# A recurrence and a feed-forward layer on one core: free PSUM banks, sums of halves on GpSimd, another order of stages

## The chip, the cores and the metric

The kernel runs on one core of a Trainium2 chip. The core has five engines, each with its own queue of instructions: TensorE (PE; its weight loads are shown apart as PEld), VectorE (DVE), ScalarE (ACT), GpSimd (POOL) and SyncE (SP), which here only issues DMAs. An engine works through its queue in order; semaphores make it wait for others. PSUM, where TensorE writes its results, has eight banks of 512 float32 values per partition.

The metric is the device time of one execution in microseconds: the median of the runs shown.

## The reference

The first part is a recurrence over 768 time steps, for 4 batches and 8 heads of width 48:

```python
for t in range(S):
    cur = np.einsum('bhd,bhe->bhde', u[None] * kt, vt)
    y[:, :, t] = np.einsum('bhd,bhde->bhe', rt, state + cur)
    state = wt[:, :, :, None] * state + np.einsum('bhd,bhe->bhde', kt, vt)
```

Its output, as 3072 rows of 384 values, goes through a feed-forward layer of width 1024:

```python
h = x @ w_in
e = np.exp(h - h_max)
solu = h * (e / np.sum(e))
ln = (solu - mean(solu)) / np.sqrt(var(solu) + 1e-06) * g_ln
return ln @ w_out
```

All inputs and the output are float32.

## The kernel before

The work is cut into 24 units: 6 chunks of 128 time steps times 4 batches (unit i has chunk i // 4 and batch i % 4). A unit goes through stages, each a small function; a stage has a short name, and one string, `ORDER`, names all stages of all units in the order in which they are recorded, with a suffix for the engine (`a` ScalarE, `d` VectorE, `p` GpSimd) or for the place in PSUM. A class `InOrder` keeps each engine's instructions in exactly that order. So each engine's queue is its part of the string, and nothing else decides the order. As the instructions are recorded in the helper, nearly all of them have its line, 87, in the profile; tile names tell the stages apart.

The stages of a unit, with the tile that each writes:

- `LW`, `LK`, `LR`, `LV`: four loads of 192 KB each, on SP, into rings of seven buffers.
- `lw`: the logarithm of the decay (ScalarE, tile lw). `cum`: two matmuls that cumulate it over the chunk (cum_ps). `ex`: its exponential, in place (ScalarE). `kp`: scaled k and r (VectorE).
- `p`, `q`: r times k times u (GpSimd). `dg`: their sum over each head (VectorE). `vb`: v as bfloat16. `dv`: v times that sum (GpSimd), the bonus of the present step.
- `krk`, `krr`: transposes (kr_ps); `kr`: their copy. `M`: scores (m_ps); `m`: their copy, on VectorE with the causal mask `keep` multiplied in, on ScalarE without, and then `sel` masks on GpSimd.
- `Y`: attention within the chunk and on the state (y_ps); `y`: its copy, on VectorE with dv added; where the copy is ScalarE's, `Y` adds dv by one more matmul (suffix `i`). `S`, `et`, `st`: the state for the next chunk.
- `X`, `xT`: the row block transposed. `H`: 24 matmuls of the hidden layer (h_ps, two banks). `e`: exponential (ScalarE). `he`: h times e (VectorE). `hq`: its square.
- `Oa`, `Ob`: the two halves of the output (o_ps). Each of the eight slices of the hidden width takes three matmuls: he with w2 (385 columns; the last sums he), e with a column of constants (one column, the sum of e), hq with a column of ones (one column).
- `sq`, `qm`, `lv`: the factor from these sums; `o`: the scaled output; `out`: its store, on SP.

Ahead of the first output the second weight is made ready: `gw` multiplies w_out by the gain g, slice by slice (w2); `mn` sums the columns by eight matmuls with a matrix of -1/1024 (mean_ps); `mc` copies that mean (mean_sb); `ce` adds it to each slice. So the mean over the hidden width is taken out of the weight. `wi` casts w_in to bfloat16. `hot` is matmuls on a zero tile whose result is not used.

PSUM is taken by tags: `s0` to `s3` of one bank, `b0` and `b1` of two; a stage's suffix names the tag, and a tag's next user waits until its last one is done. The masks and constants are made on GpSimd at the head of the program.

The functions that the change touches:

Of the kernel before, what the change touches and what calls it, by code (L numbers as in the profile page):

```python
# [8 lines left out]
F32 = mybir.dt.float32  # L9
BF16 = mybir.dt.bfloat16  # L10
AX = mybir.AxisListType.X
# [10 lines left out]
LW0 LK0 hot3.s3 LR0 LU0 LG0 lw0 LW1 cum0.b0 LK1 hot1.s3 LV0 LR1 p0 us0.s0 LW2 gs0.s3 hot2.s2 LK2 uc0 gc0 ex0 q0  # L22
LI0 LR2 lw1 kp0 LW3 cum1.b1 hot1.s3 vb0.a dg0 LV1 ex1 S0.s1 LK3 krk0.s2 p1 hot3.s3 LR3 kp1 LI1 lw2 krk1.s0 LI2
krr0 cum2.b0 LV2 kr0.d hot1.s3 LO0 M0.b1 krr1 LO1 m0.d hot3.s3 kr1.a LW4 LK4 p2 et0 ex2 M1.b1 LR4 hot4.s3 LW5
dv0 kp2 lw3 LV3 Y0.is3 m1.d vb1.p LK5 krk2.s2 y0.a q1 LR5 krr2 wi0.a cum3.b0 LW6 S1.s0 q2 dg1 X0.s3 LV4 ex3 st0
dv1 LK6 dg2 kr2.a kp3 LR6 Y1.is1 LW7 y1.a krk3.s2 LV5 et1 wi1.a krr3 X1.s1 LK7 wi2.d M2.b1 LR7 xT1.a p3 xT0.d
m2.d LW8 H0.b0 LV6 vb2.p kr3.d LK8 dv2 H1.b1 e0 st1 LR8 gw3.p LW9 gw0.p he0 S2.s1 LK9 e1 Y2.is3 q3 LR9 hot3.s2
et2 gw2.p LV7 y2.a dg3 gw7.a gw1.p X2.s2 LW10 he1 M3.b0 gw4.p LV8 lw4 gw6.p LK10 m3.d hq0.a gw5.p cum4.b1 LR10
mn0.s0 ex4 LW11 hq1.d LV9 xT2.a p4 kp4 mc0 H2.b0 lw5 ce7.d ce0.d ce3.d ce5.d krk4.s3 vb3.a cum5.b1 ce4.d e2
ce6.d krr4 S3.s2 ce1.d ce2.d st2 dv3 ex5 Oa0.s0 kr4.a q4 kp5 Y3.is1 Ob0 p5 et3 he2 lw6 y3.a krk5.s3 cum6.b1 sq0  # L30
q5 X3.s1 st3 ex6 M4.b0 qm0 krr5 xT3.d vb4.p Oa1.s2 m4.d kr5.a S4.s1 p6 lv0 kp6 M5.b0 o0.a Ob1 dg4 lw7 out0 et4
dg5 krk6.s3 m5.a dv4 cum7.b1 LK11 st4 Y4.ns0 LR11 krr6 hq2.d sq1 vb5.a H3.b0 LW12 ex7 qm1 q6 y4.d LV10 kr6.d lv1
sel5 LK12 Oa2.s1 kp7 e3 LR12 S5.s0 dv5 LV11 o1.a he3 krk7.s3 lw8 M6.b1 out1 vb6.p krr7 et5 m6.a Y5.is2 LW13 p7
kr7.d cum8.b0 LK13 dg6 Ob2 ex8 sel6 LR13 st5 X4.s3 LW14 y5.a kp8 M7.b1 sq2 dv6 xT4.a LK14 X5.s0 Y6.ns2 lw9 qm2
S6.s3 xT5.d LR14 q7 m7.a y6.d krk8.s0 LW15 cum9.b0 hq3.d X6.s2 LV12 krr8 ex9 H4.b1 p8 kr8.d lv2 kp9 et6 sel7
Oa3.s0 vb7.a st6 e4 xT6.d p9 M8.b0 dg7 S7.s3 lw10 he4 krk9.s2 q8 et7 Ob3 m8.a vb8.p o2.d cum10.b1 sq3 sel8 st7
krr9 out2 ex10 S8.s1 qm3 kr9.d LK15 H5.b0 hq4.a q9 kp10 LV13 p10 et8 lv3 st8 M9.b1 e5 krk10.s3 m9.d Y7.ns2 vb9.p
krr10 Oa4.s1 dv7 lw11 he5 o3.a cum11.b1 kr10.a out3 S9.s0 y7.d LR15 H6.b0 et9 ex11 dg8 p11 st9 kp11 Ob4 e6 dg9
X7.s3 krk11.s2 vb10.p lw12 he6 Y8.ns0 dv8 xT7.a krr11 cum12.b1 hq5.a S10.s3 q10 kr11.d H7.b0 sq4 ex12 qm4 y8.d
dv9 dg10 et10 lv4 q11 X8.s2 kp12 Oa5.s0 e7 vb11.p o4.a M10.b1 dv10 he7 Ob5 lw13 out4 xT8.a p12 LW16 S11.s1 m10.a  # L40
dg11 krk12.s2 st10 cum13.b0 et11 hq6.d krr12 sq5 ex13 H8.b1 qm5 sel10 st11 lv5 kp13 lw14 Oa6.s3 q12 e8 kr12.d
krk13.s1 p13 cum14.b0 hq7.a he8 krr13 Y9.ns2 p14 Ob6 ex14 y9.d kr13.a q13 o5.d M11.b1 Oa7.s2 dg12 out5 sq6 dv11
m11.a kp14 LK16 Y10.ns0 vb12.p X9.s1 LR16 qm6 M12.b0 xT9.a M13.b1 LV14 m12.d lw15 Ob7 LW17 m13.a vb13.p S12.s1
LK17 y10.d sel11 cum15.b0 LV15 et12 X10.s0 st12 H9.b1 ex15 dg13 dv12 xT10.a kp15 lv6 Y11.ns1 sq7 e9 krk14.s0 qm7
y11.d H10.b0 hq8.d lw16 o6.a q14 he9 X11.s1 lv7 krr14 out6 Oa8.s3 p15 e10 LR17 xT11.d kr14.d cum16.b1 o7.a dv13
S13.s1 he10 ex16 Ob8 out7 q15 LV16 hq9.a kp16 krk15.s0 sel13 LW18 M14.b0 Y12.ns2 sq8 m14.a dg14 LK18 krr15
H11.b1 qm8 p16 y12.d LR18 et13 lv8 kr15.d LV17 lw17 vb14.p st13 LW19 M15.b0 e11 Y13.ns2 krk16.s0 y13.d Oa9.s1
m15.a p17 he11 X12.s2 vb15.a krr16 sel14 cum17.b0 xT12.a dg15 Ob9 ex17 o8.d dv14 X13.s2 H12.b1 out8 sq9 xT13.a
qm9 kp17 vb16.p lv9 kr16.d H13.b0 e12 hq10.d dv15 o9.a he12 Y14.ns3 lw18 krk17.s2 out9 q16 Oa10.s0 e13 LK19
y14.d sel15 krr17 LV18 Ob10 he13 kr17.a LR19 S14.s1 LW20 hq12.a hq11.d M16.b1 LK20 M17.b0 q17 dg16 Y15.ns3 LR20  # L50
m16.a Oa11.s2 y15.d dv16 sq10 m17.d lw19 cum18.b1 p18 et14 X14.s3 Ob11 xT14.a qm10 st14 lv10 sel16 H14.b0 sq11
ex18 o10.d qm11 vb17.p dg17 out10 lv11 q18 kp18 Y16.ns3 LV19 e14 X15.s1 Oa12.s0 LW21 p19 y16.d xT15.a LV20 dg18
cum19.b1 lw20 Ob12 he14 LK21 q19 ex19 LR21 S15.s3 vb18.p sq12 o11.a LW22 kp19 krk18.s1 dv17 cum20.b0 et15 LK22
krr18 qm12 ex20 X16.s2 p20 H15.b1 out11 xT16.d kr18.a LR22 kp20 LW23 Y17.ns2 lv12 hq13.d H16.b0 e15 st15 y17.d
p21 o12.a S16.s1 he15 e16 out12 krk19.s3 q20 Oa13.s2 LV21 hq14.a he16 LK23 krr19 Ob13 LR23 lw21 kr19.d et16 LV22
X17.s0 M18.b1 st16 M19.b0 p22 S17.s3 m18.d m19.a Oa14.s1 sq13 et17 xT17.a qm13 dg19 cum21.b0 Ob14 st17 ex21
hq15.d krk20.s0 hq16.a Y18.ns3 dv18 kp21 krr20 H17.b1 sq14 lv13 sel19 y18.d lw22 kr20.d lw23 vb19.p Oa15.s3
o13.d e17 vb20.p qm14 dg20 out13 dv19 M20.b0 lv14 LV23 he17 Y19.ns0 m20.a X18.s2 Ob15 xT18.d sel20 o14.d
cum22.b1 sq15 Oa16.s2 y19.d ex22 out14 qm15 hq17.d krk21.s1 vb21.a X19.s0 kp22 q21 Ob16 lv15 q22 xT19.d cum23.b0
sq16 o15.d krr21 ex23 krk22.s0 qm16 H18.b1 p23 out15 kr21.a kp23 dv20 krr22 dg21 e18 S18.s3 kr22.d H19.b0 dv21  # L60
lv16 he18 o16.a Y20.ns1 et18 e19 out16 krk23.s0 hq18.d M21.b1 Oa17.s2 y20.d m21.a st18 krr23 he19 Ob17 sel21
kr23.a Oa18.s1 dg22 sq17 q23 Y21.ns3 hq19.d X20.s0 M22.b1 xT20.a qm17 vb22.p M23.b0 y21.d lv17 Ob18 m23.d dv22
m22.a S19.s0 sq18 X21.s3 dg23 sel22 H20.b1 et19 o17.d xT21.d out17 vb23.p qm18 st19 Y22.ns2 dv23 e20 H21.b0
y22.d lv18 he20 Oa19.s3 e21 o18.d X22.s0 Y23.ns2 hq20.d xT22.a out18 Ob19 y23.d Oa20.s1 sq19 qm19 he21 lv19
X23.s0 H22.b1 xT23.d hq21.a H23.b0 e22 Oa21.s2 he22 e23 Ob20 he23 hq22.a Ob21 sq20 o19.a qm20 hq23.d Oa22.s0
lv20 out19 sq21 o20.d Oa23.s3 qm21 out20 lv21 Ob22 Ob23 sq22 qm22 o21.d lv22 sq23 out21 qm23 o22.d lv23 out22
o23.d out23
# [27 lines left out]
def kernel(  # L95
# [34 lines left out]

    def bank(shape, dtype, slot, name):
        return psum.tile(shape, dtype, tag=slot, name=name)
# [31 lines left out]
    pool.memset(halves, 0.0)  # L164
    pool.memset(halves[0:2, :], 1.0)
    pool.affine_select(out=halves[0:2, :], in_=halves[0:2, :], compare_op=ALU.is_ge, fill=0.0, base=0,
                       pattern=[[1, C]], channel_multiplier=-64)
    pool.affine_select(out=halves[0:2, :], in_=halves[0:2, :], compare_op=ALU.is_gt, fill=0.0, base=64,
                       pattern=[[-1, C]], channel_multiplier=64)
    off_blocks = consts.tile([C, HP, 2], BF16)  # L170
    pool.memset(off_blocks, 0.0)
    pool.memset(off_blocks[0:2], -30000.0)
    pool.affine_select(out=off_blocks[0:2], in_=off_blocks[0:2], compare_op=ALU.not_equal, fill=0.0, base=0,
                       pattern=[[0, HP], [-1, 2]], channel_multiplier=1)
# [10 lines left out]
    for j in range(max(NLW, NKP)):  # L185
        if j < NLW:
            dve.memset(lw_t[j][:, :, D:], 0.0)
        if j < NKP:
# [5 lines left out]
    keep = consts.tile([C, C], BF16)  # L194
    pool.memset(keep, 1.0)
    pool.affine_select(out=keep, in_=keep, compare_op=ALU.is_gt, fill=0.0, base=0,
                       pattern=[[1, C]], channel_multiplier=-1)
# [12 lines left out]
    e_t = ring("e", NWK, [128, KF, C], BF16)  # L210
    he_t = ring("he", NWK, [128, KF, C], BF16)
# [11 lines left out]


# [63 lines left out]
    def centre(f, x):  # L288
        (dve if x == "d" else pool).tensor_add(out=w2[:, f, :DM], in0=w2[:, f, :DM], in1=mean_sb)
# [32 lines left out]

    def v_cast(i, x):
        copy = {"a": act.copy, "p": pool.tensor_copy}[x]
        copy(out=vb_t[i % NLW], in_=v_t[i % NIO][:, :, :D])

    def bonus_sum(i, x):
        dve.reduce_sum(out=dg_t[i % NWK], in_=q_t[i % 3], axis=AX)
# [41 lines left out]
    def scores_mask(i, x):  # L370
        m = m_t[i % NWK]
        pool.affine_select(out=m, in_=m, compare_op=ALU.is_gt, fill=0.0, base=0,
                           pattern=[[0, H], [1, C]], channel_multiplier=-1)

    def attend(i, x):
        L = live[i]
        c, b = units[i]
        m, kr, vb = m_t[i % NWK], kr_s[i % NKP], vb_t[i % NLW]
        y_ps = L["y_ps"] = bank([C, DM], F32, x[-2:], "y_ps")
        first = True  # L380
        if x[0] == "i":
            pe.matmul(y_ps, lhsT=ident, rhs=dv_t[i % NKP].rearrange("t h d -> t (h d)"), start=True, stop=False,
                      skip_group_check=True)
            first = False
        if c > 0:
# [160 lines left out]
```

## Time and profile before

| | us |
|---|---|
| median of three runs | 158.17 (158.06 to 163.34) |
| the profiled execution: its span, the only time that is given for it | 156.5 |
| what the median has beyond that span | 1.7 |
| TensorE busy | 138.6 (89%) |
| VectorE busy | 129.8 (83%) |
| ScalarE busy | 118.4 (76%) |
| GpSimd busy | 103.1 (66%) |
| first output matmul starts | 38.7 |
| last output matmul ends | 152.1 |
| DMA queue of SP | 26.75 MB, 75.4% of 16 DMA engines' span |

The span is from the first to the last instruction. A row of the groups gives busy time and the mean of one instruction from its start to its end; since an instruction may start before the one ahead of it has ended, above all on TensorE, means times counts add up to more than the busy time. "PEclk" is the granted TensorE clock in tenths of full speed. The chain of waits is followed back from the last instruction: at each step what released it, or the instruction ahead of it on its engine.

### The profile page before, as it was taken

To read this page: it belongs to the slowest core of one execution; us is meant where nothing else is said; L and a number is where in the kernel's file an instruction comes from. 1 tells how busy PE (TensorE), PEld (TensorE's weight loads), DVE (VectorE), ACT (ScalarE), POOL (GpSimd) and SP (SyncE) were. 2 spreads that over 40 slices of the span, in tenths; PEclk is the share of its full clock that TensorE was granted. 3 is DMA by queue.
4 is the path that set the end of the run, shared out by engine and by line. 5 is a ranking of instruction groups with operands and counts; after the bars stand their busy time and mean duration, and the time that the engine had idled before them with its cause. 6 is when DMAs were issued, how large, how long until landed. Compare 5 with 4: busy or idle time off the path is not lost.

```text
span 156.5 us, 5279 instructions
## 1 busy us (share of the span) xinstructions
PE 138.6 (89%) x2161; PEld 108.1 (69%) x2161; DVE 129.8 (83%) x227; ACT 118.4 (76%) x241; POOL 103.1 (66%) x131
## 2 busy tenths in 40 slices
PE   3879859449599999999999999999999989999980
PEld 1244447218378788887879788887978778798750
DVE  5054777737999999999989989999999999997652
ACT  4171786616589998989998998999979869655941
POOL 7442858995809999895999977399249782860000
PEclk9999999857999999999999999999999999999999
DMA  4999999999999979999559696596999611011024
GB/s 95 195 215 237 265 354 298 211 226 175 208 224 187 225 155 241 178 228 222 124 121 224 168 194 159 136 211 142 222 212 225 170 57 53 4 50 54 0 105 151
DMA packets 104825, 27.08 MB, mean 173 GB/s; under 512 B 100313, under 2 KB 104418, under 8 KB 104802
## 3 DMA queue, kind: packets, MB, share of 16 engines
q1 hardware_dynamic: 104802, 26.75, 75.4%
q8 instruction: 17, 0.28, 0.7%
q14 instruction: 6, 0.05, 0.1%
HBM read 22.03 MB, written 4.72 MB: 171 GB/s over the span
## 4 chain that ended last, share of the span: by engine, by line
PE 65%; SPq 10%; DVE 9%; POOL 5%; DMA 5%; issue 3%; ACT 1%; DVEq 0%; POOLq 0%
PE o_ps L87 23%; PE h_ps L87 17%; SPq L87 10%; PE kr_ps L87 5%; DMA wout_f<-in_moe_w_out_dram 5%; PE s_ps L87 5%; PE y_ps L87 5%; POOL w L87 5%; PE m_ps L87 4%; PE cum_ps L87 3%; DVE w L87 3%; PE x_ps L87 2%; DVE o L87 1%; DVE hq L87 1%; PE mean_ps L87 1%
## 5 line engine op out<-in xcount | busy, mean ns | idle before, releaser
L87 PE MATMUL o_ps<-w,he 128*128 128x385 bf16 x192 | 45.9, 325 | 1.9 <-DVE w L87 1.9
L87 PE MATMUL h_ps<-xT,win_sb 128*128 128x128 bf16 x576 | 36.5, 222 | 0.7 <-DVE xT L87 0.7
L87 PEld LDWEIGHTS <-win_sb 128*128 128x128 bf16 x576 | 34.0, 99 | 1.1 <-ACT xT L87 0.7
L87 DVE TENSOR_TENSOR he<-h_ps,e 128x1024 bf16<-128x1024 f32 x24 | 29.2, 1217 | 3.1 <-ACT e L87 2.7
L87 PE MATMUL o_ps<-inv_col,e 128*128 128x1 bf16 x192 | 31.7, 165 | 0.0
L87 POOL TENSOR_TENSOR p<-kr_in 128x384 bf16<-128x384 f32 x24 | 24.5, 1023 | 10.9 <-DMA kr_in<-in_r_dram 10.9
L87 PE MATMUL o_ps<-one_col,hq 128*128 128x1 bf16 x192 | 31.3, 163 | 0.0
L87 POOL TENSOR_TENSOR dv<-vb,dg 128x384 bf16<-128x384 bf16 x24 | 20.5, 856 | 13.8 <-DVE dg L87 11.9
L87 ACT ACTIVATE e<-h_ps 128x1024 bf16<-128x1024 f32 x24 | 24.5, 1020 | 6.6 <-PE h_ps L87 6.4
L87 DVE TENSOR_TENSOR kp<-cum_ps,kr_in 128x768 bf16<-128x768 f32 x24 | 22.8, 948 | 7.5 <-ACT cum_ps L87 7.3
L87 PEld LDWEIGHTS <-hq 128*128 128x128 bf16 x192 | 18.5, 96 | 12.8
L87 POOL TENSOR_TENSOR q<-p,u_bc 128x384 bf16<-128x384 bf16 x24 | 23.7, 990 | 1.6 <-DMA kr_in<-in_k_dram 1.5
L87 ACT ACTIVATE cum_ps<-cum_ps 128x768 f32<-128x768 f32 x24 | 19.2, 802 | 3.7 <-PE cum_ps L87 3.4
L87 PEld LDWEIGHTS <-kp 128*128 128x128 bf16 x272 | 17.5, 99 | 3.9 <-DVE kp L87 1.2
L87 PEld LDWEIGHTS <-e 128*128 128x128 bf16 x192 | 18.4, 96 | 2.4 <-issue 2.0
L87 POOL TENSOR_SCALAR_AFFINE_SELECT m<-m 128x1024 bf16<-128x1024 bf16 x14 | 15.7, 1119 | 6.4 <-ACT m L87 4.0
L87 PE MATMUL kr_ps<-ident,kp 128*128 128x128 bf16 x192 | 18.7, 225 | 0.9 <-DVE xT L87 0.5
L87 PEld LDWEIGHTS <-he 128*128 128x128 bf16 x192 | 18.4, 96 | 1.0
L87 ACT CAST m<-m_ps 128x1024 bf16<-128x1024 f32 x14 | 14.2, 1011 | 1.0 <-PE m_ps L87 1.0
L87 DVE TENSOR_REDUCE dg<-q 128x8 f32<-128x384 bf16 x24 | 12.9, 540 | 1.4 <-POOL q L87 1.4
L87 ACT COPY kr<-kr_ps 128x1024 bf16<-128x1024 bf16 x10 | 10.1, 1014 | 4.1 <-PE kr_ps L87 4.1
L87 DVE TENSOR_TENSOR m<-m_ps,keep 128x1024 bf16<-128x1024 f32 x10 | 12.1, 1215 | 0.9 <-PE m_ps L87 0.9
(82 smaller groups left out, 276.4 us busy)
## 6 DMA issues: line engine op xcount, KB each, us to landing
w_in<-in_w_dram SPq DMA_DIRECT2D x24, 192.0 KB, 3.6
kr_in<-in_k_dram SPq DMA_DIRECT2D x24, 192.0 KB, 3.7
kr_in<-in_r_dram SPq DMA_DIRECT2D x24, 192.0 KB, 3.7
v_in<-in_v_dram SPq DMA_DIRECT2D x24, 192.0 KB, 3.6
out_dram<-o SPq DMA_DIRECT2D x24, 192.0 KB, 2.0
win_f<-in_moe_w_in_dram SPq DMA_DIRECT2D x3, 512.0 KB, 5.6
wout_f<-in_moe_w_out_dram SPq DMA_DIRECT2D x2, 768.0 KB, 8.5
u_row<-in_u_dram SPq DMA_DIRECT2D x1, 1.5 KB
```

Source lines behind the costliest of these rows:

```text
L87: made = make(*args, **kwargs)
```

## The change

- PSUM is one tile of eight banks. A stage's suffix is the number of its first bank, and any one or two neighbouring free banks will do. Waits follow from the parts of the tile that are read and written.
- `ce` on VectorE computes a slice anew as w_out times gain plus the mean, which it reads from PSUM; on GpSimd it is as before. Four of the eight slices go to each. The gains go to VectorE (4), ScalarE (2) and GpSimd (2), where seven were GpSimd's.
- `ea`, new, for 17 units: GpSimd adds the upper half of e to the lower (128x512 values), and the output takes four matmuls instead of eight for the sum of e.
- `qh`, new, for 12 units: GpSimd adds the two halves of each head in q (192 values per partition), and `dg` sums half as many.
- `v_cast` may be VectorE's (6 units; 12 GpSimd, 6 ScalarE). The masks are stages in the order (`ih`, `ik`).
- The order is another one: which unit's stage stands where, which engine has which copy (masked scores copies: VectorE 15 for 10; outputs: ScalarE 19 for 11; attention copies: ScalarE 7 for 5), and where loads and stores stand.

```diff
-LW0 LK0 hot3.s3 LR0 LU0 LG0 lw0 LW1 cum0.b0 LK1 hot1.s3 LV0 LR1 p0 us0.s0 LW2 gs0.s3 hot2.s2 LK2 uc0 gc0 ex0 q0
...
-dv1 LK6 dg2 kr2.a kp3 LR6 Y1.is1 LW7 y1.a krk3.s2 LV5 et1 wi1.a krr3 X1.s1 LK7 wi2.d M2.b1 LR7 xT1.a p3 xT0.d
-m2.d LW8 H0.b0 LV6 vb2.p kr3.d LK8 dv2 H1.b1 e0 st1 LR8 gw3.p LW9 gw0.p he0 S2.s1 LK9 e1 Y2.is3 q3 LR9 hot3.s2
...
+LW2 LU0 ik0 lw2 hot5.4 cum2.0 LW1 lw1 us0.7 ih0 LW3 lw3 cum3.2 LR2 uc0 ex2 LK2 p2 LV2 vb2.p kp2 hot4.4 krk2.6 krr2
...
+M4.0 m4.a et1 LI0 S0.5 et0 wi0.d m3.d LO1 wi2.p H1.6 e1 gw5.a H2.0 e2 H0.2 LO0 gw2.a q4 qh4 dg4 qh3 dg3 gw4.p
+gw7.p LV3 vb3.p dv3 sel4 LW6 e0 gw6.d st1 LV4 vb4.p he1 lw6 dv4 gw1.d LW5 gw0.d gw3.d mn0.4 mc0 ce5.p ce6.p
+Y3.i7 ce4.p he2 st0 he0 cum6.0 y3.a ce7.p hot1.5 X3.6 lw5 xT3.a ce3.d LK6 LR6 p6 Y4.n5 LR5 LK5 ce2.d hq0.a ex6
+LW7 cum5.2 H3.6 p5 y4.d ex5 ce1.d ce0.d Oa0.5 kp6 krk6.1 krr6 S4.0 hq1.d Oa1.4 kp5 krk5.3 krr5 X4.2 Ob1 e3 he3
...
+    banks = psum.tile([128, 8 * 512], F32, name="ps")
     def bank(shape, dtype, slot, name):
-        return psum.tile(shape, dtype, tag=slot, name=name)
+        size = 1
+        for d in shape[1:]:
+            size *= d
+        first = int(slot) * 512
+        if dtype == BF16:
+            part = banks[:, first:first + size // 2].bitcast(BF16)
+        else:
+            part = banks[:, first:first + size]
...
     def centre(f, x):
-        (dve if x == "d" else pool).tensor_add(out=w2[:, f, :DM], in0=w2[:, f, :DM], in1=mean_sb)
+        if x == "p":
+            pool.tensor_add(out=w2[:, f, :DM], in0=w2[:, f, :DM], in1=mean_sb)
+        else:
+            dve.scalar_tensor_tensor(out=w2[:, f, :DM], in0=wout_f[:, f, :], scalar=gr[:, f:f + 1], in1=ps["mean"],
+                                     op0=MULT, op1=ADD)
...
+    def bonus_half(i, x):
+        q = q_t[i % 3]
+        pool.tensor_add(out=q[:, :, :D // 2], in0=q[:, :, :D // 2], in1=q[:, :, D // 2:])
...
     def bonus_sum(i, x):
-        dve.reduce_sum(out=dg_t[i % NWK], in_=q_t[i % 3], axis=AX)
+        part = slice(0, D // 2) if i in halved else slice(0, D)
+        dve.reduce_sum(out=dg_t[i % NWK], in_=q_t[i % 3][:, :, part], axis=AX)
...
+    def hidden_add(i, x):
+        e = e_t[i % NWK]
+        pool.tensor_add(out=ea_t[i % NWK], in0=e[:, :KF // 2, :], in1=e[:, KF // 2:, :])
...
-            pe.matmul(o_ps[:, DM + 1:DM + 2], lhsT=e[:, f, :], rhs=inv_col, start=False, stop=False,
-                      skip_group_check=True)
+            if i not in added:
+                pe.matmul(o_ps[:, DM + 1:DM + 2], lhsT=e[:, f, :], rhs=inv_col, start=False, stop=False,
+                          skip_group_check=True)
+            elif f % 2 == 0:
+                pe.matmul(o_ps[:, DM + 1:DM + 2], lhsT=ea_t[i % NWK][:, f // 2, :], rhs=inv_col, start=False, stop=False,
+                          skip_group_check=True)
```

## The prediction

> **What bounds the kernel now.** I read the span in slices first: when is TensorE full, and at which clock?
>
> ```profile
> PE   3879859449599999999999999999999989999980
> DVE  5054777737999999999989989999999999997652
> PEclk9999999857999999999999999999999999999999
> ```
>
> TensorE is full from slice 12 on (45 us) and not before. So there are two terms: when the full stretch begins, and how much work lies in it. Next the busy times of PE, PEld, DVE, ACT and POOL by stretch (length first; then granted clock, DMA share, GB/s):
>
> ```profile
> 38.70:41.90 3.20, 1.31 (x17) 0.87 (x14) 3.20 (x5) 2.27 (x5) 3.12 (x5) 1.00 1.12 218
> ...
> 45.30:117.30 72.00, 71.98 (x1263) 59.94 (x1260) 69.26 (x114) 67.39 (x141) 56.73 (x66) 1.00 0.87 187
> 117.30:126.90 9.60, 9.09 (x148) 7.16 (x146) 9.60 (x19) 8.20 (x19) 8.72 (x10) 1.00 0.71 166
> ```
>
> From 45 to 117 us TensorE rests 0.02 us, but VectorE is at 96%: a second bound close behind, which takes over from 117 to 127. At 39 to 42 TensorE is 41% busy. Why it starts late is in the chain of waits (start, length, what):
>
> ```profile
> 17.12 7.74 DMA wout_f<-in_moe_w_out_dram
> ...
> 24.95 2.46 POOL w L87 x2
> ...
> 29.49 4.91 POOL w L87 x4
> ...
> 34.44 1.13 PE mean_ps L87 x3
> ...
> 36.39 4.85 DVE w L87 x7
> 41.28 0.56 PE o_ps L87 x6
> ```
>
> w_out lands at 24.9, GpSimd multiplies seven of its eight slices by the gain (1.245 us each) until 34.4, TensorE takes the column mean, ScalarE copies it (0.48), VectorE adds it to eight slices. The first output matmul starts at 38.7, but the matmuls wait for slices until 41.3.
>
> **TensorE's work, step by step.** A stage's price is its piece in the full part of the chain: hidden layer 1.34 us, half of the output 0.83, cumulation 0.33, transposes 0.45, scores 0.33, attention 0.37, state 0.46. With these, the order before holds 17.9 us ahead of the first output matmul and 108.3 from it on. The trace took 38.7 to 152.1, 113.4: so 5.1 us are lost there, 1.9 of them waiting for centred slices. One output step in the timeline prices the removed matmuls:
>
> ```profile
> 42.13 0.32 PE L87 MATMUL o_ps<-w,he 128*128 128x385 bf16 x1
> ...
> 42.29 0.17 PE L87 MATMUL o_ps<-inv_col,e 128*128 128x1 bf16 x1
> ...
> 42.31 0.16 PE L87 MATMUL o_ps<-one_col,hq 128*128 128x1 bf16 x1
> ...
> 42.34 0.32 PE L87 MATMUL o_ps<-w,he 128*128 128x385 bf16 x1
> ```
>
> The row says 0.165 us for one column, but matmuls are pipelined: start to start it is 0.026. The change removes 17 x 4 = 68 of them: 68 x 0.026 = 1.8 us, not the 11 us that the row suggests. Two more units add their bonus by an identity matmul (2 x 0.16), two warm-ups go (2 x 0.21). The rest of the gain on TensorE is order: the new one puts H3, two more attentions, a score and a cumulation ahead of the first output and one state behind it, so 19.9 us ahead (2.0 more) and 104.4 from it on: 3.9 less than now.
>
> **When the output can start.** In the new order 18 instead of 15 unit loads are queued on SP ahead of w_out's end. At the saturated 205 GB/s a load of 192 KB is 0.96 us; w_out moves from 24.9 to 27.7 us. The last part of w_in is then there by about 23.4 (2 us start, 18 loads, half of the 8.6 us that remain for the weights out of 24.9), its VectorE copy (0.69) ends at 24.1, and the first hidden layer runs 24.4 to 25.8. On VectorE: exp (1.02, ScalarE) until 26.9, product of unit 1 until 28.1, three gains until 29.3, product of unit 2, a state (0.55), product of unit 0 until 32.2, two centrings, a y (0.55), two centrings: 35.2. ScalarE has hq0 done by 33.7. The mean (gains of ScalarE and GpSimd end by 29.3, eight matmuls at 0.16) is there at 30.7 and is covered. GpSimd starts its four centrings after v, dv and a mask of units 3 and 4, at 33, and ends at 37; they are needed only by the second half of a unit, after Oa0, Oa1 and two transposes (38). I take 36.0 for the first output matmul, 0.8 for semaphores, against 38.7 now, and no wait of 1.9 inside it. If the hidden layers or the masks come late, nothing covers VectorE's chain, and it is 1 for 1 on the end.
>
> Rows that the trace lacks, with ends: a gain on VectorE 0.35 (xT copy) to 0.61 (o), taken 0.4; a centring with PSUM input 0.55 (y) to 0.95 (kp), taken 0.6; on GpSimd 0.86 (dv) to 1.25 (gain), taken 0.99 as q; the w_in cast on GpSimd 0.54 (v) to 1.43 (v by elements), taken 1.4. Together with 1 us either way in the landing of w_out, -1.5 to +2.5 us on the start.
>
> **The other engines.** Sums by row means: VectorE 140.0 now, 138.5 after (15 for 10 masked scores copies +6.1, 5 for 13 outputs -4.9, six v casts +2.4, four gains +1.6, centring -2.5, twelve halved sums -2.9, the rest -1.3). The page has 129.8 for 140.0, as starts overlap ends, a factor 0.927. After the last centring 108.0 are left now (from 41.2) and 105.4 in the new order, from 35.2: an end at 140.6 for VectorE alone, much the same as TensorE's 36.0 + 104.4. ScalarE stays (133.3 to 133.8 by row means). In the built program its separate wait instructions go from 32 to 68, since reads of one bank by two engines are now waited for one by one; between nothing and 0.06 us each that is 0 to 2.2 us, hidden in ScalarE's 24% of idle time. TensorE's 37 waits on its own earlier work go: 0 to 0.55 once (17.5 us), taken 0.
>
> GpSimd takes over 17 sums of e. Ends for one: 0.99 (q has 384 elements, this 512) to 1.32 (q by elements), taken 1.3; and 12 halves of q, 0.29 (a 128x128 cast) to 0.99, taken 0.55. Less five masks, six casts and five gains, it goes from 103 to 124 us. The sum runs beside VectorE's product and square (1.2 + 0.7) and is ready before them if GpSimd is free. Behind it in the queue stand p, q and dv of later units.
>
> The same engine slows VectorE, as the tile view says (min/median/max ns):
>
> ```profile
> L87 DVE TENSOR_TENSOR hq<-he x14: 673/686/1409, 31.1 to 148.5; 128x1024 bf16<-128x1024 bf16 x14
> ```
>
> The 1.41 us one, at 124.3, starts with two q on GpSimd, 2.23 for 0.91 each. Mean 0.82 for 0.68: 2.0 us in all now; with a fifth more on GpSimd and ten more copies and gains exposed, 1 to 3 more, taken 1, in VectorE's slack of about 4.
>
> A rule against the change stands in the Trainium skill, "GPSIMD Engine Reference", Engine selection: elementwise work belongs on VectorE, GpSimd is about twice as slow with two inputs. Its per-element model (2.6 cycles at 1.2 GHz) would make a sum of 512 elements 1.1 us, an estimate from that page: 17 of them 3 us less on GpSimd than I take, and the forecast the same, since it is not on the path.
>
> SP: 40 unit loads now stand ahead of the first store, 44 before. A load behind a store waits for it. The tightest is the v of unit 22 behind the store of unit 12, used 1.4 us of TensorE work later with 3.6 us to land: 2 to 3 us late on GpSimd, with the sums of 16, 18 and 17 behind it. Output 16 comes 7.6 us of TensorE work later, which hides it.
>
> **The sum.** 36.0 + 104.4 + 5.1 lost as now (the 1.9 of waits for slices goes; I put as much for stalls in the first units after it, where VectorE has products, squares and copies of several units queued back to back) = 145.5; tail as now, 156.5 - 152.1 = 4.4; span 149.9. The median of the runs lies 1.7 over the profiled span of 156.5: **151.6 us**.
>
> **Rivals.** *VectorE and GpSimd hold TensorE up*: both are near full, the start slips to 37.5 and twice the stalls (10.2) arise: 37.5 + 104.4 + 10.2 + 4.4 + 1.7 = 158.2. For: the 117 to 127 stretch and the 1.41 us square. Against: 0.02 us of rest over 72 us at 96% of VectorE.
>
> *GpSimd becomes the bound, slower than before*: what it waited for between 45 and 140 us starts
>
> ```profile
> POOL dv L87 <- DVE dg L87: 11.2, 6, 4.5
> POOL p L87 <- DMA kr_in<-in_r_dram: 5.2, 3, 3.0
> POOL m L87 <- ACT m L87: 4.0, 3, 3.0
> ```
>
> and sums to 22.6. After its last centring (37.7) it has 95.3 us left; with the same 22.6 of waits the last sum ends at 155.6, two output halves (1.6), tail and 1.7 follow: 163.3. It decides once the waits exceed 145.5 - 1.6 - 37.7 - 95.3 = 10.9. Against: most of those waits were for want of work.
>
> *The early start does not come*: the first output stays at 38.7, and only the shorter rest remains: 38.7 + 104.4 + 5.1 + 4.4 + 1.7 = 154.3.
>
> **Chances.** Forecast 0.55 (148.5 to 154.0, by the start's ends and 3 to 7 us of stalls), no early start 0.10, held up 0.18, GpSimd bound 0.17. Two per cent, about what a measurement of this kernel tells from no change, is 155.0 to 161.3: faster 0.62, same 0.21, slower 0.17. The range reaches from the forecast's lower end into the held-up case: 148.5 to 160.0.
>
> **What would show it.** Right: first output matmul at 35 to 37, its run without gaps of a microsecond, TensorE full from 42, GpSimd sums of 1.0 to 1.3 us never the releaser of o_ps, output halves of 0.78. Wrong: TensorE waiting for the sum of e or for VectorE in the middle stretch, or w2 ready later than 38.

## The result, and the profile after

The changed kernel takes 154.22 us (median of four runs, 153.98 to 154.78) against 158.24 for the kernel before on the same chip: ratio 0.9748, 95% interval 0.971 to 0.9785. It is faster; 151.6 had been forecast. Medians are over all runs; ratios leave out the runs that were disturbed on the chip, which are four of six for two of the kernels below (the gains alone, and the sums for the last units), so that only the ratio is given there, with a wide interval.

The page's slices of the changed kernel, in the form that was shown for the kernel before:

```profile
PE   6777598968999999999998999999799999999970
DVE  5029968899999999998999999999999999988940
POOL 7268986799909994899999997799889979973600
PEclk9959969999999999999999999999999999999998
```

TensorE is full from slice 10 (38 us) on, but for slices 21 and 28 (80 to 84 and 107 to 110). VectorE is full from slice 8 almost to the end. The clock dips twice ahead of 23 us, where it had dipped from 27 to 39. Now the busy times of PE, PEld, DVE, ACT and POOL by stretch (then granted clock, DMA share, GB/s):

```profile
38.20:42.00 3.80, 3.75 (x57) 2.94 (x57) 3.80 (x4) 3.27 (x5) 3.60 (x4) 1.00 1.09 216
...
45.30:117.30 72.00, 70.45 (x1187) 57.58 (x1185) 70.45 (x116) 65.85 (x144) 65.31 (x74) 1.00 0.96 205
117.30:126.90 9.60, 9.60 (x173) 8.65 (x172) 9.56 (x15) 8.10 (x17) 8.59 (x10) 1.00 0.18 66
```

The first row is the start of the output: 3.75 of 3.80 us busy, where TensorE was 41% busy before. In the 72 us of the middle it now rests 1.55 us (0.02 before), VectorE is at 98% (96%), and the DMA engines are busy for 0.96 of the time at 205 GB/s (0.87 at 187). So three resources stand within a few per cent of each other in the middle stretch.

| | before | after |
|---|---|---|
| profiled execution: span | 156.5 | 152.4 |
| first output matmul starts | 38.7 | 38.2 |
| from there to the end of the last output matmul | 113.4 | 109.4 |
| TensorE's work in it, by the prediction's prices | 108.3 | 104.4 |
| lost in it | 5.1 | 5.0 |
| from there to the end of the span | 4.4 | 4.8 |

The 4.1 us of span are 0.5 at the start and 4.0 behind it, less 0.4 at the tail. The start was to give 2.7. The chain of waits up to it (start, length, what):

```profile
13.35 3.79 DMA kr_in<-in_k_dram
...
19.25 3.19 PE ps L86 x28
...
22.46 1.24 DVE m L86
...
25.59 1.06 ACT win_sb L86
...
26.70 1.47 PE ps L86 x23
28.17 0.02 issue
28.19 1.03 ACT e L86
29.23 0.02 issue
29.25 1.22 DVE he L86
30.47 2.40 DVE w L86 x3
32.87 1.13 DVE he L86
```

The chain no longer passes through w_out's landing, GpSimd's gains and the mean. It runs through the first units' own stages to the hidden layer at 26.7, and then, behind one exponential, on VectorE alone: product, three gains, two more products, centrings. From there VectorE is the path to the first output.

### The profile page after: what moved, and what is told of

It is laid out like the page before. It is cut to its first block, busy times and chain, and to the rows that moved or that the text cites. A ratio compares the mean times of both kernels' runs of the same rounds, so it can differ in the third digit from the quotient of the medians.

```text
span 152.4 us, 5172 instructions
## 1 busy us (share of the span) xinstructions
PE 136.4 (90%) x2093; PEld 105.5 (69%) x2093; DVE 131.8 (87%) x227; ACT 120.0 (79%) x247; POOL 119.0 (78%) x149
## 4 chain that ended last, share of the span: by engine, by line
PE 53%; DVE 23%; SPq 8%; ACT 6%; issue 3%; DMA 2%; POOL 1%; DVEq 0%; POOLq 0%
PE ps L86 53%; SPq L86 7%; DVE he L86 6%; DVE m L86 4%; DVE kp L86 4%; DVE w L86 3%; DMA kr_in<-in_k_dram 2%; DVE kr L86 1%; DVE hq L86 1%; DVE y L86 1%; DVE st L86 1%; ACT ps L86 1%; ACT o L86 1%; DVE dg L86 1%; ACT win_sb L86 1%
## 5 line engine op out<-in xcount | busy, mean ns | idle before, releaser
L86 PE MATMUL ps<-w,he 128*128 128x385 bf16 x192 | 44.5, 325 | 1.0 <-DVE w L86 0.7
L86 PE MATMUL ps<-xT,win_sb 128*128 128x128 bf16 x576 | 35.5, 219 | 1.1 <-DVE qm L86 0.8
L86 PE MATMUL ps<-one_col,hq 128*128 128x1 bf16 x192 | 31.5, 164 | 0.0
L86 DVE TENSOR_TENSOR he<-ps,e 128x1024 bf16<-128x1024 f32 x24 | 29.1, 1214 | 1.6 <-ACT e L86 1.6
L86 DVE TENSOR_TENSOR kp<-ps,kr_in 128x768 bf16<-128x768 f32 x24 | 22.8, 951 | 7.7 <-DMA kr_in<-in_k_dram 4.9
L86 ACT ACTIVATE e<-ps 128x1024 bf16<-128x1024 f32 x24 | 24.5, 1021 | 3.1 <-PE ps L86 2.0
L86 POOL TENSOR_TENSOR ea<-e 128x512 bf16<-128x512 bf16 x17 | 20.0, 1181 | 6.4 <-ACT e L86 5.7
L86 ACT ACTIVATE ps<-ps 128x768 f32<-128x768 f32 x24 | 19.1, 799 | 5.1 <-PE ps L86 4.3
L86 PEld LDWEIGHTS <-he 128*128 128x128 bf16 x192 | 18.4, 96 | 4.0
L86 DVE TENSOR_TENSOR m<-ps,keep 128x1024 bf16<-128x1024 f32 x15 | 18.2, 1216 | 1.2 <-PE ps L86 1.0
L86 PE MATMUL ps<-ident,kp 128*128 128x128 bf16 x192 | 16.5, 227 | 1.6 <-POOL p L86 1.1
```

What stands on the lines that cost most here:

```text
L86: made = make(*args, **kwargs)
```

## The experiments

A first group takes the change apart on the side of the kernel before, a second on the side of the kernel after; a third tries to use what they showed.

### PSUM as one tile

The old order, in the old places of PSUM, with PSUM as one tile:

```diff
-krk0.s2 krr0 cum2.b0 kr0.d M0.b1
+krk0.2 krr0 cum2.4 kr0.d M0.6
```

> The kernel before, its order unchanged; only PSUM is one tile of eight banks, with the old tags on fixed banks (s0 to s3 on 0 to 3, b0 on 4 and 5, b1 on 6 and 7). If the new way of waiting on PSUM costs or gains nothing by itself (my theory): 158.2 within 0.5. If TensorE's 37 waits on its own earlier work cost it something, up to 2 us less, 156.2 to 157.5. If the more numerous ScalarE waits cost: up to 2 us more.

Measured: 158.41 us, ratio 0.9988 [0.9959, 1.0018], no change. The other form of PSUM and of its waits is neither gain nor loss by itself; what matters is the order that it allows.

### The sums of e, in the old order

The kernel before with `hidden_add`, each sum right behind its exponential, in the 17 units that the change names:

```diff
-e5 krk10.s3
+e5 ea5.p krk10.s3
```

> The kernel before, its order unchanged, but for the same 17 units GpSimd adds the halves of e (right after e in the order) and the output takes four matmuls fewer. Theory that the full stretch is TensorE's: 68 x 0.026 = 1.8 us less, 156.4. Rival, that VectorE and GpSimd hold TensorE up: GpSimd gets 17 x 1.18 = 20 us more, slows VectorE's squares and queues ahead of dv, so 158.2 or more.

Measured: 163.7 us, ratio 1.0281 [1.0203, 1.0359]: slower by 4.5 us. In its profile the first output starts at 40.6 instead of 38.7; that is not the sums' work, as the first of them runs at 64.9 (w_out had landed 1.1 us later in this execution). At the 33rd output matmul of 385 columns, at 64.8, it is 1.1 us behind the kernel before, at the last one 5.2. Between the first output and the last one 10.3 us are lost instead of 5.1. The waits of this kernel over the whole span (what waited for what: sum, times, longest):

```profile
POOL ea L86 <- ACT e L86: 9.8, 9, 3.0
...
PE y_ps L86 <- POOL m L86: 1.6, 1, 1.6
...
DVE y L86 <- POOL dv L86: 1.4, 2, 0.9
```

GpSimd works in order. It stands nine times before a sum whose exponential is not there, 9.8 us in all, with the next units' p, q and dv queued behind. TensorE then waits for a masked score of GpSimd (1.6 us) and VectorE for a dv (1.4 us), two waits that the trace of before does not have. The chain of waits runs through GpSimd's sums and bonuses, for instance here:

```profile
64.93 1.15 POOL ea L86
...
66.53 0.79 POOL dv L86
```

This is the mechanism of the forecast's rival "GpSimd becomes the bound", in the old order. That the time is near the rival's price (163.3) is chance: the price was summed up for the new order.

### Gains and centring, in the old order

The kernel before with the gains and the centring on the engines that the change gives them, each in its old place:

```diff
-gw3.p gw0.p gw2.p gw7.a gw1.p gw4.p gw6.p gw5.p
+gw3.d gw0.d gw2.a gw7.p gw1.d gw4.p gw6.d gw5.a
-ce7.d ce0.d ce3.d ce5.d ce4.d ce6.d ce1.d ce2.d
+ce7.p ce0.d ce3.d ce5.p ce4.p ce6.p ce1.d ce2.d
```

and with the new `centre`, which computes VectorE's slices from w_out, gain and the mean in PSUM.

> The kernel before, its order unchanged, but gains and centrings on the engines that the new kernel uses for them (gains: VectorE 4, ScalarE 2, GpSimd 2; centring: VectorE 4 from PSUM, GpSimd 4). Theory that the end follows the first output one for one: the gains end some 3.5 us earlier, the first output without waits starts at 36 to 37 instead of 38.7 with 1.9 of waits, 154 to 155.5. Rival, that VectorE is the bound and the start matters little: it has about 1 us less to do in all, 157 to 158.2.

Measured: 154.25 us, ratio 0.9721 [0.9666, 0.9776]. This part alone gives all that the whole change gives. Its first output starts at 34.19, 4.5 us earlier than before, and its last ends 4.8 earlier. VectorE's weight work in its timeline (start, length, engine, line, operation, shape, count):

```profile
25.06 0.75 DVE L85 TENSOR_SCALAR w<-wout_f,gr 128x384 bf16<-128x384 f32 x2 [0.29 <-DMA wout_f<-in_moe_w_out_dram]
...
31.96 2.17 DVE L85 SCALAR_TENSOR_TENSOR w<-wout_f,gr,mean_ps 128x384 bf16<-128x384 f32 x4
```

The first gains start as w_out lands, at 0.4 each; the centrings are over at 34.1, where the old ones ended at 41.2. The clock, at half from 30.4 to 37.3 us in the kernel before and full here, is at most a small part of this: of the old weight chain only the last three matmuls of the mean run on TensorE in that stretch, for 1.13 us, where all eight take 1.33 here.

The gains alone, with all eight centrings as before:

```diff
-gw3.p gw0.p gw2.p gw7.a gw1.p gw4.p gw6.p gw5.p
+gw3.d gw0.d gw2.a gw7.p gw1.d gw4.p gw6.d gw5.a
```

> The kernel before, its order unchanged, with only the gains spread (VectorE 4, ScalarE 2, GpSimd 2); the mean is still copied and added on VectorE to all eight slices. Theory that GpSimd's 8.6 us of gains were the path: most of the 4.4 us of gains and centring together comes from this part, first output at 35, 155. Rival, that centring from PSUM on two engines is what counts: 157 to 158.

Measured: ratio 0.9746 [0.9648, 0.9845], not separated from the run above; it rests on two runs (153.76 and 155.18) of six that reach 160.05. The profiled execution (156.64) starts its first output at 34.64, but the second slice comes late:

```profile
34.64 0.32 PE L85 MATMUL o_ps<-w,he 128*128 128x385 bf16 x1 [0.59 <-DVE w L85]
...
37.81 0.32 PE L85 MATMUL o_ps<-w,he 128*128 128x385 bf16 x1 [2.82 <-DVE w L85]
```

VectorE adds the mean to the eight slices from 32.7 to 38.0. So the output runs on from 37.8, where the kernel before had 41.3 and the one with both parts 34.2, and the 17th output matmul of 385 columns (47.72) is 1.7 us ahead of before, against 6.2 with both. By this profile the new centring is worth as much of the start as the gains; by the two runs of the ratio the gains alone reach about the same time. How the 4 us are shared stays open.

### Taking parts out of the changed kernel

The changed kernel once more, unchanged, as the measure of the others:

> The new kernel, unchanged, beside the other three: 154.2 again. Its profile shows how far the first output (38.2 us in the first profile, where the granted clock dipped to 0.5 and 0.6 in two early slices) moves from execution to execution: if the dips made it late, 36.5 to 37 without them.

Measured: 154.18 us, ratio 0.9731 [0.9683, 0.9779], first output at 38.16, the last output matmul of 385 columns at 147.23 as in the first profile. The clock dipped again in the same place: 0.56 on average from 18.4 to 21.9 us (0.51 in the first profile). So this run does not show the start without the dip; the next one does.

Without the sums of e:

```diff
-out0 ea5.p Y6.i5
+out0 Y6.i5
```

> The new kernel without GpSimd's sums of e: all units take eight one-column matmuls for the sum again. Theory that TensorE is the bound: 1.8 us more than the new kernel, 156.0. Rival, that VectorE and GpSimd are the bound: GpSimd is relieved of 20 us and VectorE of held squares, 154.2 or less.

Measured: 154.12 us, ratio 0.9714 [0.9667, 0.9762], the same time although TensorE has 68 matmuls more. What this kernel waited for between 45 and 125 us, and two pieces of its chain:

```profile
POOL p L83 <- DMA kr_in<-in_r_dram: 4.8, 3, 3.1
POOL p L83 <- DMA kr_in<-in_k_dram: 3.3, 1, 3.3
POOL vb L83 <- DMA v_in<-in_v_dram: 2.3, 3, 1.7
```

```profile
53.80 4.89 DMA kr_in<-in_r_dram
...
68.37 4.86 DMA kr_in<-in_r_dram
```

The changed kernel has no wait for a load in that stretch; its chain runs through VectorE and ScalarE where this one runs through the loads. The loads in this chain were issued late: SP's issues ahead of the first one begin at 50.9, when a scaled copy has freed a buffer of the ring, and follow each other until 53.8; the load then takes 4.9 us (median of all here: 3.8). How much of that is the rate of the DMA engines and how much the seven buffers of the ring was not separated.

In the profiled execution without the sums the output started 1.2 us earlier (36.97), though the changed kernel has no sum ahead of 56 us. What differs is the granted clock (the third number from the end), here from 18.4 to 21.9 us in the changed kernel and then in this one:

```profile
18.40:21.90 3.50, 3.15 (x28) 2.07 (x28) 2.86 (x4) 1.37 (x3) 3.01 (x5) 0.51 0.98 302
```

```profile
18.40:21.90 3.50, 3.02 (x46) 1.99 (x47) 3.40 (x6) 2.19 (x4) 2.96 (x4) 1.00 0.94 296
```

The 28 matmuls of the changed kernel's chain that start at 19.25 took 3.2 us, the same matmuls 2.2 here. The hidden layer came 0.7 us earlier (26.0), and the three gains behind it took 1.90 us instead of 2.48. So the earlier start goes with the clock of this execution, not with the sums; one profile of each does not tell how often it comes.

Of 192 matmuls with 385 columns, the 17th came 1.5 us ahead of the changed kernel's and the 33rd 0.5 us. No sum's matmul lies between these (the first stands at 60.9 us in the changed kernel), so about 1 us was given back where the chain waits for the load at 53.8; from there on this kernel falls back another 1.4 us, for which the 68 matmuls (1.8) are enough.

Without the halves of the bonus sum:

```diff
-q4 qh4 dg4
+q4 dg4
```

> The new kernel without the halves of q: VectorE sums all 384 values in all units (12 x 0.2 = 2.4 us more for it), GpSimd has 6.5 us less. Theory that VectorE is the close second bound: 154.2 to 156. Rival, that GpSimd's queue is the bound: 153 to 154.

Measured: 154.15 us, ratio 0.9723 [0.9673, 0.9772], the same. VectorE is busy for 132.8 instead of 131.8 us, GpSimd for 112.4 instead of 119.0. One engine's microsecond is bought with 6.6 of the other's, and neither is felt.

With the old gains and the old centring in the new order:

```diff
-gw5.a gw2.a gw4.p gw7.p gw6.d gw1.d gw0.d gw3.d
+gw5.a gw4.p gw7.p gw6.p gw2.p gw1.p gw0.p gw3.p
-ce5.p ce6.p ce4.p ce7.p
+ce5.d ce6.d ce4.d ce7.d
```

> The new kernel with the old way of the second weight: seven gains on GpSimd in a row, one on ScalarE, the copied mean added on VectorE to all eight slices. Theory that the whole gain is this part: the first output comes 5 us later, and the time is 158 to 160, no better than the kernel before. Rival, that order, sums and halves bring something of their own: below 157.

Measured: 162.5 us, ratio 1.0235 [1.0178, 1.0293]: slower than before. GpSimd's queue in its timeline, and what VectorE then waited for:

```profile
27.37 8.56 POOL L84 TENSOR_SCALAR w<-wout_f,gr 128x384 bf16<-128x384 f32 x7 [2.28 <-DMA wout_f<-in_moe_w_out_dram]
```

```profile
DVE w L84 <- ACT mean_sb L84: 8.2, 1, 8.2
```

Seven gains in a row, 8.56 us, and VectorE stands 8.2 us; the first output starts at 47.4. Part of that is the clock, granted at 0.50 from 34 to 47 us: the eight matmuls of the mean took 2.98 us, where they take 1.49 in the run below that draws the weight path together. So the new order needs the new centring: it puts w_out later, and has nothing else to do while the weight is made ready.

### Is the start on the path one for one?

Three kernels try to start the output earlier. In the changed kernel, three of VectorE's gains put ahead of the product of unit 1:

```diff
-e0 gw6.d st1 LV4 vb4.p he1 lw6 dv4 gw1.d LW5 gw0.d gw3.d mn0.4
+e0 gw6.d gw1.d gw0.d gw3.d st1 LV4 vb4.p he1 lw6 dv4 LW5 mn0.4
```

> The changed kernel with one edit in the order: three of VectorE's four gains (slices 1, 0, 3) stand right behind the fourth (slice 6), ahead of a state and of the product of unit 1. They then run at 28.0 us, where VectorE waits 0.74 us for the exponential anyway, and where GpSimd does its own two gains; in the changed kernel they run at 30.4 beside GpSimd's v cast, bonus and mask and take 2.48 us for three. Theory (GpSimd's work of those kinds makes VectorE's gains slow, and the first output's start is on the path to the end one for one): the three gains take 1.2 to 1.4 us, the product of unit 2 follows that of unit 1 directly, the first output matmul starts at 36.2 to 37.0 instead of 38.2, and the median falls to 152.3 to 153.2. Rival A (any work of GpSimd slows these gains, its gains too): they take 2.4 us again, the start gains 0.4 us or less, the median stays at 154.0 to 154.4. Rival B (the start is not what sets the end, VectorE's total is): the start falls to 36.5 and the median stays at 154.0 to 154.4.

Measured: 153.1 us, ratio 0.9684 [0.9654, 0.9713]. Five of its six runs (152.81 to 153.63) lie below all ten of the changed kernel (153.72 to 154.78); the intervals of the ratios just touch (0.9713 and 0.971). One piece of its chain and the three gains in its timeline:

```profile
19.62 9.79 DMA wout_f<-in_moe_w_out_dram
```

```profile
29.43 1.57 DVE L84 TENSOR_SCALAR w<-wout_f,gr 128x384 bf16<-128x384 f32 x3 [1.09 <-DMA wout_f<-in_moe_w_out_dram]
```

The expectation was half wrong: the gains could not run at 28.0, because the second half of w_out landed only at 29.4. But they took 1.57 us for 2.48: they were over at 31.0, when GpSimd's bonus had just begun (30.87) and its mask had not (31.65). The profile is of the slowest of the six runs (154.16) and has its first output at 37.93, so it does not show where the typical run's 1.1 us are.

In the old order with the new centring, the whole weight path drawn together:

```diff
-gw0.d he0 gw2.a gw7.p gw1.d he1 gw4.p lw4 gw6.d hq0.a gw5.a cum4.b1 mn0.s0
+gw0.d gw1.d he0 gw2.a gw7.p gw6.d gw4.d he1 gw5.a lw4 hq0.a mn0.s0 cum4.b1
-hq1.d kp4 ce0.d ce3.d krk4.s3 krr4 ce1.d ce2.d Oa0.s0
+ce0.d ce3.d ce1.d ce2.d kp4 hq1.d Oa0.s0 krk4.s3 krr4
```

> The kernel before with the changed kernel's gains and centring (that alone gave 154.25 and a first output at 34.2), and now its weight path drawn together in the order: slice 4 is VectorE's too (GpSimd has one gain left), the gains stand ahead of the product of unit 1, the mean's eight matmuls ahead of a cumulation, and VectorE's four centrings ahead of a square and a scaled copy, with the transposes of unit 4 behind the first half of the output. Theory (the end follows the first output one for one): mean at about 28.5 us, VectorE's centrings from 30.7 to 32.9, first output at 33.0, 1.2 us earlier, and 152.8 to 153.4. Rival (VectorE's total, or stages pushed behind the output, hold the rest back): the start falls to 33 and the median stays at 154.0 to 154.6, with the lost time from first output to last matmul going from 4.9 to 6 us.

Measured: 155.79 us, ratio 0.9818 [0.9761, 0.9876], 1.5 us slower by the median than without these moves (0.9721, up to 0.9776, so the intervals just touch); the first output starts at 37.07, later instead of earlier. Its timeline says why:

```profile
33.33 2.19 DVE L85 SCALAR_TENSOR_TENSOR w<-wout_f,gr,mean_ps 128x384 bf16<-128x384 f32 x4 [1.89 <-ACT mean_sb L85]
```

```profile
36.44 0.34 PE L85 MATMUL cum_ps<-lw,uti_neg 128*128 128x384 bf16 x1 [1.97 <-DVE kp L85]
```

Two queues were overlooked. The copy of the mean stood on ScalarE behind an exponential that now came after the mean, and VectorE's centring, though it reads the mean from PSUM and not the copy, started only when the copy ended, by a semaphore of ScalarE's for which it waits in this program. And the cumulation of unit 5, which stands in TensorE's queue ahead of the output, needs the PSUM place that the scaled copy of unit 4 frees, which had been put behind the centrings: 1.97 us of TensorE.

Last, the changed kernel with the three gains early and the product of unit 2 behind the centrings:

```diff
-ce4.p he2 st0 he0 cum6.0 y3.a
+ce4.p he0 st0 y3.a
-hq0.a ex6 LW7 cum5.2 H3.6 p5 y4.d ex5 ce1.d ce0.d Oa0.5 kp6 krk6.1 krr6 S4.0 hq1.d Oa1.4 kp5 krk5.3 krr5 X4.2
+hq0.a LW7 cum5.2 H3.6 p5 y4.d ex5 ce1.d ce0.d he2 Oa0.5 cum6.0 ex6 kp5 krk5.3 krr5 hq1.d Oa1.4 kp6 krk6.1 krr6 S4.0 X4.2
```

> The changed kernel with the three gains put forward as in the run before, and also the product of unit 0 ahead of that of unit 2, which goes behind VectorE's four centrings; the stages that hang on unit 2's bank (cumulation, exponential, scaled copy, transposes of unit 6) go behind the first output. So 1.2 us of VectorE's work leaves the path to the first output, and none of it is removed. Theory (the rest from first output to last matmul is 109.4 us wherever the start lies, so the end follows the start): first output at 36.7 to 37.0, the last output matmul starts at 146.0 to 146.5, median 151.8 to 152.4, against 153.0 with the gains alone put forward. Rival (VectorE is full from 29 to 46 us, and that backlog, not the place of one stage in it, sets the end): the start comes earlier as said and the rest grows by as much, to 110.5; median 152.8 to 153.3. Slower than 153.5 would mean that TensorE now waits in its queue for the stages that were put behind.

Measured: 156.09 us, ratio 0.9867 [0.9835, 0.9899]. The start came as said, at 36.97. The rest grew, and the time with it. Two lines of its timeline:

```profile
38.68 0.80 ACT L84 ACTIVATE ps<-ps 128x768 f32<-128x768 f32 x1 [1.67 <-PE ps L84]
```

```profile
38.98 0.62 PE L84 MATMUL ps<-ident,kp 128*128 128x128 bf16 x8 [0.38 <-DVE kp L84]
```

ScalarE now waits 1.67 us for the cumulation that was put behind, and TensorE for a scaled copy. The 192 output matmuls of 385 columns, in the order of their time, show what became of each start (us, from the timelines):

| matmul | before | gains and centring alone | after | after without sums | gains early | product of unit 2 behind |
|---|---|---|---|---|---|---|
| 1st | 38.69 | 34.19 | 38.20 | 36.97 | 37.93 | 36.97 |
| 17th | 49.44 | 43.22 | 47.25 | 45.75 | 46.83 | 47.50 |
| 33rd | 63.70 | 57.48 | 60.69 | 60.15 | 60.26 | 60.94 |
| 65th | 86.44 | 81.18 | 84.13 | 83.55 | 83.70 | 84.39 |
| 97th | 105.97 | 100.68 | 103.59 | 103.90 | 103.67 | 104.37 |
| 161st | 142.29 | 137.52 | 139.62 | 140.15 | 139.70 | 140.43 |
| 192nd | 151.77 | 147.00 | 147.23 | 148.12 | 147.31 | 148.03 |

With the product of unit 2 put behind, the output is 1.2 us ahead of the changed kernel at the first matmul and 0.25 behind at the 17th, nine microseconds later. The kernels without sums and with early gains lose their advance (1.5 and 0.4) between the 17th and the 97th. The kernel with gains and centring alone is 6.2 us ahead of the kernel before at the 17th and 4.8 at the end, and between 45 and 125 us its longest wait was this:

```profile
POOL p L85 <- DMA kr_in<-in_r_dram: 10.7, 4, 4.5
```

So the theory "the end follows the start one for one" falls. An earlier start counts as long as everything behind it can come earlier too. Beyond that, some of it is given back: where the chain of waits runs through loads (three pieces without the sums, one with gains and centring alone: 4.59 us of a load of the decay at 62.05), or at once to the stages that were pushed aside. Of the last kernel's 3.0 us over the one before it, the two profiles show 0.7 at the last output and 1.1 in the tail; the rest isn't settled, since one of the two profiles is of an untypically slow run.

### Sums where nothing stands behind them

The kernel with gains and centring alone, and sums only for units 20 to 23:

```diff
-e20 H21.b0
+e20 ea20.p H21.b0
```

> The kernel before with the changed kernel's gains and centring, and sums of e on GpSimd for the last four units (20 to 23) alone, each right behind its exponential; behind the first of them GpSimd's queue holds only the last few bonus products. Theory (a sum costs nothing where nothing is queued behind it, and saves four one-column matmuls of 0.026 us): 16 matmuls fewer, 0.4 us, 153.7 to 154.0, against 154.25 without the sums. Rival (a sum of 1.2 us stands between exponential and output and delays the last units, where each stage waits for the one ahead): 154.5 to 155.5.

Measured: ratio 0.9593 [0.9495, 0.9691], from two runs (150.62 and 152.72) of six that reach 156.51. The interval overlaps that without the sums (0.9666 to 0.9776). It speaks against the rival, a loss; that the sums help here by the 0.4 us expected isn't shown.

## Why the prediction was right, and where it was not

**The verdict** was right and the time, 154.2, was in the range, but 2.6 us over the forecast. By its number it is the third rival, *the early start does not come* (154.3, given 0.10): the start moved by 0.5 us and the shorter rest gave the other part. Of the 2.6 us, 2.2 are the start and 0.4 the tail.

**The step that failed is "I take 36.0 for the first output matmul".** It came at 38.2. Three of its terms were too small.

- *The last part of w_in by 23.4, the first hidden layer from 24.4 to 25.8.* It landed at 25.2, and the layer ran from 26.70 to 28.17. The estimate counted loads, and the last one came 1.8 late. It left out the queues: ScalarE's cast of w_in ran only at 25.59, behind two copies of k and r and two of x, the last of which waited for a chain that starts with a load of k at 13.35. And it left out the clock, which was at 0.51 on that chain: in the execution at full clock, with the same landing (25.2), ScalarE's cast ran at 24.54 and the layer from 26.0. So 1.6 of the 2.3 us are the landing and the cast behind it, 0.7 ScalarE's late cast. The prediction's own words, that nothing covers VectorE's chain if the hidden layers come late, name what happened.
- *w_out at 27.7.* Its second half was issued at 19.6 and took 9.6 us, so 29.2; in the run with early gains it ended at 29.4. In the changed kernel that lay under the late hidden layer.
- *Three gains until 29.3, at 0.4.* One took 0.41, the other three 2.48. The timelines of VectorE (its last line is the last of the three by itself) and of GpSimd show them side by side:

```profile
27.63 0.41 DVE L86 TENSOR_SCALAR w<-wout_f,gr 128x384 bf16<-128x384 f32 x1
...
30.39 2.48 DVE L86 TENSOR_SCALAR w<-wout_f,gr 128x384 bf16<-128x384 f32 x3
...
31.62 1.24 DVE L86 TENSOR_SCALAR w<-wout_f,gr 128x384 bf16<-128x384 f32 x1
```

```profile
29.96 0.50 POOL L86 CAST vb<-v_in 128x384 bf16<-128x384 f32 x1 [0.25 <-DMA v_in<-in_v_dram]
30.55 0.94 POOL L86 TENSOR_TENSOR dv<-vb,dg 128x384 bf16<-128x384 bf16 x1
31.45 1.21 POOL L86 TENSOR_SCALAR_AFFINE_SELECT m<-m 128x1024 bf16<-128x1024 bf16 x1
```

The third and fourth gain took 0.99 and 1.24: the last one starts at 31.62, just behind the mask, and ends at 32.86, 0.2 behind the mask's end; the one before it ends as far behind the bonus (31.70 for 31.49). That is 1.3 us more than taken, on the path. The prediction had the effect, as 1 us somewhere in VectorE's slack; it fell where there was none. The run that moves the gains out of GpSimd's way had 1.57 for the three, and 1.1 us less time by its median; its profile, of its slowest run, starts the output only 0.3 earlier, so the link between the two isn't shown. The Trainium skill, "SBUF — State Buffer", SBUF: two separate sides, says that VectorE, in some of its modes, and GpSimd take turns at a pair of ports, each for a whole instruction; the gain that lasts until the mask is over agrees with that. The first gain, 0.41 in the midst of GpSimd's own gain (27.25 to 28.50), was not held, but in the run with early gains another one was: 0.66, ending 0.2 behind GpSimd's gain (30.43 for 30.21). What decides this is not shown.

The first and third miss make 3.6 us. Behind the gains, 0.6 came back, as each of VectorE's instructions starts some 0.08 us ahead of the end of the one before it, which the prediction's sum of durations left out here; and of the 0.8 taken for semaphores 0.05 were needed. That leaves the measured 2.2. The other terms of the step held: centring from PSUM 0.60 (taken 0.6), on GpSimd 0.83 (0.99), ended at 37.7 (37); the cast on GpSimd 1.04 (1.4). There is no wait of 1.9 us inside the first output.

**The rest behind the start** came out as summed, 109.4 for 109.5: work 104.4, lost 5.0 for 5.1. The 5.0 is partly luck: 1.9 of stalls were put in by a guess, for the first units; TensorE rested 0.2 us there, and 1.55 in the middle stretch, which was to be full. The reading of the 3.9 us as a gain was too simple, too. Of them, 2.0 were only moved ahead of the start, where VectorE is the path; what they cost there was not measured. The other 1.8, the 68 removed matmuls, are nowhere in the median: the kernel without the sums is as fast. What the forecast left out is that loads stand close behind in the middle stretch (loads and stores take 0.96 of the DMA engines' time): they are on the chain of the kernel without sums and of the one with gains and centring alone. The new order and the new way with the weight do not add: the second takes the old order to 154.25; the new order with the old way is at 162.5.

**The sums of e and the halves.** A sum took 1.18 on average (taken 1.3), a half 0.55 (0.55). The Trainium skill's model ("GPSIMD Engine Reference", Elementwise — side-by-side cycle accounting) makes 1.1 of a sum, an estimate, near the median of 1.15 here; the mean lies above that by one sum of 1.60 beside VectorE's square. From the tile view, count and min/median/max in ns of the sums, and of VectorE's squares, which run beside them:

```profile
L86 POOL TENSOR_TENSOR ea<-e x17: 1147/1153/1600, 56.1 to 143.1; 128x512 bf16<-128x512 bf16 x17
```

```profile
L86 DVE TENSOR_TENSOR hq<-he x15: 673/772/1581, 38.9 to 144.5; 128x1024 bf16<-128x1024 bf16 x15
```

The squares take 0.89 on average for 0.82 before, 1 us over 15 of them; without the sums they take 0.84. GpSimd is busy for 119.0 us (103.1 before); its durations add up to 123.2, for 124 expected by row means.

**The rival of GpSimd** did not come. What GpSimd waited for between 45 and 140 us:

```profile
POOL ea L86 <- ACT e L86: 5.0, 3, 3.2
POOL dv L86 <- DVE qm L86: 3.6, 1, 3.6
POOL dv L86 <- DVE vb L86: 2.7, 1, 2.7
```

With two smaller ones these sum to 13.3 us, above the 10.9 at which the rival was to decide. (That point takes 37.7 for the end of GpSimd's centrings, the sum for the start 37; it was 37.7.) It did not: the last sum starts at 143.1 and ends 3 us ahead of the last output matmul of 385 columns, and no output waits for one. A wait for an exponential that is itself late with TensorE's path is no load on GpSimd, and the point counted it as one. The mechanism is real, as the sums in the old order show.

**The rival of VectorE** is half there: the chain of waits runs through VectorE and ScalarE at 75 to 83 and 90 to 110 us, and TensorE rests 1.55 us in the middle, not the ten that the rival asked for. "TensorE full from 42" was right but for that. Two signs that the prediction named for being wrong came, both small: TensorE waited for VectorE in the middle stretch, and the last centring ended at 38.15, later than 38.

**Smaller terms.** The six casts of v on VectorE took 0.64 on average (0.4 taken). The tail took 4.8 (4.4 taken); the constant outside the span 1.7, as taken. TensorE's waits on itself and ScalarE's longer list of wait instructions cost nothing that can be measured: the kernel before with PSUM as one tile is as fast as with tags. No load behind a store was waited for between 45 and 125 us.

## What to carry to other kernels

When a chain that readies a weight ends last, spread that chain over the engines before anything else: here that alone was worth the whole change. The start of a stage is found by asking, on each engine's queue, what stands ahead of the instruction and what that waits for; adding up durations and landing times gave 2.2 us too little. And where TensorE, VectorE and the loads are each within a few per cent of full, taking 1.8 us from one of them may buy nothing, as here: test each part alone before it is kept. Before an earlier or later start is put down to an edit, compare the granted clock ahead of it: here a dip of 3.5 us, present in one execution and not in another, went with a first output 1.2 us later.

## What the runs showed of the hardware

- VectorE's elementwise instructions on SBUF took up to three times as long beside GpSimd's: a gain of 128x384 0.41 alone, up to 1.24; a square of 128x1024 0.67 alone, 1.58 where it starts 0.05 us behind a mask. In the changed kernel each of the eight squares that took over 0.70 ended 0.54 to 0.55 us behind the end of an instruction of GpSimd that had begun before it; one behind whose start a bonus began 0.04 us later took 0.67. GpSimd's own took longer too: a bonus of 128x384 0.94 for 0.83, a mask 1.21 for 1.09, a sum of e up to 1.60 for 1.15. Copies of k and r out of PSUM, of the same size as the squares, kept to 0.67 to 0.69 beside GpSimd's products, bonuses, casts, masks and sums. Centrings that read the mean from PSUM stayed at 0.60 to 0.61, beside GpSimd's centrings.
- The granted clock fell to half for 3 to 14 us at a time, at places that differ from run to run. In the kernel before it fell where TensorE waits for the weight (0.77 on average at 30 to 45 us); in the changed kernel at 18.4 to 21.9 us, with TensorE busy for 3.15 of these 3.50; in the profiles of the kernel with gains and centring alone and of the one without sums not at all ahead of the last output. What makes it fall is not shown. With the old gains in the new order:

```profile
PEclk9999599975559999999999999999999999999998
```
